# An expert kernel on one core: the first expert's start is put in another order

## The chip, the core and the metric

The kernel runs on one core of a Trainium2 chip. Its time is the device time of one execution in microseconds (us). TensorE (PE) multiplies, VectorE (DVE) and ScalarE (ACT) copy, convert and apply functions, GpSimd (POOL) computes too and issues the gathers, SyncE (SP) issues nearly all other DMAs. Each engine works through its own list of instructions in a fixed order and waits in it; so one instruction that waits holds up all that stand behind it in that list.

## The reference

Three stages on 2304 tokens of 512 numbers, in float32: an attention (two kinds, added), a dense product `((x @ w1) * (x @ w2)) @ w3 @ w_out`, and a mixture of eight experts in which each token goes to one of them. Cut to the part around the change:

```python
logits = x @ w_gate
e_idx = np.argmax(logits, axis=1)
probs = softmax(logits)
gate_w = probs[np.arange(N), e_idx]
eom = 1.0 / (1.0 + np.exp(-(x @ w_output_gate)))
for e in range(E):
    mask = e_idx == e
    h = np.maximum(x[mask] @ w1[e], 0.0)
    ye = h @ w2[e]
    out[mask] = gate_w[mask, None] * eom[mask, e, None] * ye
```

## The kernel before

Every float32 product is made of three matmuls (`mm3`, L418 to L420) of high and low parts: high by high, high by low, low by high. A weight piece of 128 x 1024 is loaded raw, ScalarE casts its high part (L737), and VectorE or GpSimd subtracts to give the low part (L739); `ew_load` and `ew_split` do this, four pieces for each of an expert's two matrices.

The dense stage works in groups of 384 tokens. `g2_step` makes its result y for 128 tokens and one half of the 512 columns: 24 matmuls into a PSUM bank, a copy into an SBUF buffer (L475 for the lower half, by ScalarE) and a store into the DRAM tensor `yd` (L476, by SyncE). Upper halves go to a second tensor, `yh`, too.

When all logits are known, tables of the tokens of each expert are made (`route_pos`, `route_tok`, `route_rank`, `route_idx`), and the experts follow in order of size, with `CAPS[0]` = 352 tokens in the first, that is three blocks of 128, 128 and 96. `x_gather` fetches the rows of an expert's tokens by an indirect DMA (L694, on GpSimd, one for each block), `x_prep` transposes them on PE (L712) and converts them to high and low (L716, ScalarE and VectorE). `ga_part` and `ga_step` multiply by the first matrix, in eight products f = 0 to 7 of 128 outputs each; `ga_out` applies ReLU (L765). `gb_step` multiplies by the second matrix. `o_step` scales a block by the gates and scatters it.

For the first expert the rows come in two parts, since the last lower halves of y are made last. The upper columns are gathered from `yh` (`x_gather(0, 1)`) while PE still makes lower halves. From them come the *upper halves* of six products of the first matrix (six matmuls each, without closing the sums). The lower columns are gathered from `yd` (`x_gather(0, 0)`) when the last store has landed, and then come the *lower halves* of those six products and the last two products whole. Between the upper halves and the lower rows stands `route_gtab` (L599): the matmul that puts the gates of the last group into the table; `route_gates` (L655, then L637 and L638) sums and picks the gates, which are first used when the first expert's output is scaled, in the second expert.

Order is written out by hand there: `ordered` chains PE's steps, `behind` makes a weight load wait for the first rows, `after` puts work behind a conversion, and a scheduler fills in the order on the other engines from its own estimate of times. PSUM: `at_psum` hands out two banks for transposes and small products, four banks hold f = 0 to 3, and two banks shared with `g2_step` hold f = 4 and 5.

Of the kernel before, what the change touches and what calls it, by code (L numbers as in the profile page):

```python
# [48 lines left out]
def attention_moe_kernel(ctx: ExitStack, tc: tile.TileContext, q, k, vw_in, v4_in, w1, w2, w3, w_out,  # L49
# [407 lines left out]

    def g2_step(g, t, hf):
        ps = ps2.tile([P, 512], F32, name="g2", tag="g2")
        n0, n1 = HALF[hf], HALF[hf + 1]  # L460
        for f in range(KF):
            c = slice(P * t, P * t + P)
            mm3(ps[:, 0:HN[hf]], hts[g, f][0][:, c], hts[g, f][1][:, c], wc[:, f, 0, n0:n1], wc[:, f, 1, n0:n1],
                f == 0, f == KF - 1)
        r0 = G * g + P * t
        n = DM // 2
        yn[0] += 1
        y = yb[:, yn[0] % 3, :]
        if hf == 1:
            if t == 0:  # L470
                lg[g] = mt([P, CPG, 2 * E], F32, "lg", bufs=2)
            nc.vector.tensor_copy(lg[g][:, t, :], ps[:, n:n + 2 * E])
            nc.vector.tensor_copy(y, ps[:, 0:n])
        else:
            nc.scalar.copy(out=y, in_=ps[:, 0:n])  # L475
        store = nc.sync.dma_start(out=yd[r0:r0 + P, n0:n0 + n], in_=y)  # L476
        if hf == 1:
            nc.sync.dma_start(out=yh[r0:r0 + P, :], in_=y)
        return store


    def at_psum():
        if psb is None:
            return psa.tile([P, 512], F32, name="at", tag="at")
        return psb.tile([P, 512], F32, name="tr", tag="tr", bufs=2)

    psb = None
    acc = mt([P, E], F32, "acc")
    tab = mt([P, 3, E, NC], F32, "tab")
# [257 lines left out]
    def ga_part(r, f, k0, k1, first, last):  # L747
        C = CAPS[r]
        hi, lo = ew[r, 0, f // 2]
        if first:  # L750
            if f < 4 or last:
                gp[f] = psb.tile([P, 512], F32, name="g1", tag="g1", bufs=4)
# [255 lines left out]
    for i in range(2):  # L1008
        ew_load(0, 0, i)
    ordered(g2_step, NG - 1, 0, 0)  # L1010
    rows = x_gather(0, 1)
    behind(rows, ew_load(0, 0, 2))
    behind(rows, ew_load(0, 1, 0, early[:, 0]))
    ew_split(0, 0, 0)
    ordered(g2_step, NG - 1, 1, 0)
    for b in range(NBLK[0] - 1):
        ordered(x_prep, 0, b, KD // 2, KD)
    ew_split(0, 0, 1)
    store = ordered(g2_step, NG - 1, 2, 0)
    with tc.issue_after(store.ins):  # L1020
        ew_load(0, 1, 1, early[:, 1])
    rows = x_gather(0, 0)
    behind(rows, ew_load(0, 0, 3))
    last = ordered(x_prep, 0, NBLK[0] - 1, KD // 2, KD)
    with after(last):
        ew_split(0, 0, 2)
        route_gate(NG - 1)
        rhs = mt([P, CPG, 2 * E * NC], F32R, "rhs", tag="W15")
        for c in range(CPG):
            gate_rhs(NG - 1, c, rhs[:, c])  # L1030
        ew_split(0, 1, 0)
    for f in range(6):
        ordered(ga_part, 0, f, KD // 2, KD, True, False)
    ordered(route_gtab, NG - 1, rhs)
    route_gates()
    with tc.issue_after(rows.ins):
        first = ew_split(0, 1, 1)
    for b in range(NBLK[0]):
        last = ordered(x_prep, 0, b, 0, KD // 2)
    with after(last):  # L1040
        ew_split(0, 0, 3)
    for i in range(2, 4):
        behind(rows, ew_load(0, 1, i, early[:, 2] if i == 2 else None))
    for r in range(E):
        for f in range(KF):
# [4 lines left out]
            if f % 2 == 0:  # L1050
                if r > 0:
                    ew_split(r, 1, f // 2)
                elif f < 4:
                    with after(last):
                        ew_split(r, 1, 2 + f // 2)
                if r + 1 < E:
                    ew_load(r + 1, 0, f // 2)
            if f % 2 == 1 and r > 0 and f // 2 < NBLK[r - 1]:
                ordered(o_step, r - 1, f // 2)
# [74 lines left out]
```

## Time and profile before

| what | us |
|---|---|
| median of three runs | 733.2 (728.99 to 734.5) |
| the profiled execution | 731.68 |
| its span, first to last instruction | 729.9 |
| PE busy | 695.8 (95%) |
| VectorE busy | 422.8 (58%) |
| GpSimd busy | 340.7 (47%) |
| ScalarE busy | 286.1 (39%) |

The span is what the profiler saw from the first to the last instruction; the execution's own time is 1.78 us longer. The mean granted clock of TensorE is 0.992 of its full 2.4 GHz; the lower level is 1.2 GHz, shown as 0.50. Matmuls overlap, so the length of one (0.32 us for 352 columns) is longer than the step from one to the next. A bracket behind an instruction tells how long its engine was idle before it and what ended that. DMA transfers themselves are not instructions: a row of SP or of an indirect DMA is the time of issuing it.

### The profile page before, as it was taken

To read this page: it belongs to the slowest core of one execution; us is meant where nothing else is said; L and a number is where in the kernel's file an instruction comes from. 1 tells how busy PE (TensorE), PEld (TensorE's weight loads), DVE (VectorE), ACT (ScalarE), POOL (GpSimd) and SP (SyncE) were. 2 spreads that over 40 slices of the span, in tenths; PEclk is the share of its full clock that TensorE was granted. 3 is DMA by queue.
4 is the path that set the end of the run, shared out by engine and by line. 5 is a ranking of instruction groups with operands and counts; after the bars stand their busy time and mean duration, and the time that the engine had idled before them with its cause. 6 is when DMAs were issued, how large, how long until landed. Compare 5 with 4: busy or idle time off the path is not lost.

```text
span 729.9 us, 14702 instructions
## 1 busy us (share of the span) xinstructions
PE 695.8 (95%) x5710; PEld 666.0 (91%) x5711; DVE 422.8 (58%) x884; ACT 286.1 (39%) x664; POOL 340.7 (47%) x339
## 2 busy tenths in 40 slices
PE   5887999999999999999999999989999999999995
PEld 3677989899999999999999999979999999999994
DVE  8997889854545446253242343575776656765830
ACT  3455435563444136135212121345353444544510
POOL 6975567873562157032011020166474655765511
PEclk9999999999999999999999999999999999999998
DMA  8978546363243043111100101665454744545301
GB/s 327 265 251 250 217 124 214 108 196 119 83 126 102 30 109 97 52 40 44 37 30 1 44 1 44 207 246 180 154 175 145 257 159 162 208 169 198 116 25 42
DMA packets 38266, 97.73 MB, mean 134 GB/s; under 512 B 6019, under 2 KB 12931, under 8 KB 38193
## 3 DMA queue, kind: packets, MB, share of 16 engines
q1 hardware_dynamic: 34768, 86.82, 36.5%
q0 software_dynamic: 3424, 9.93, 3.8%
q8 instruction: 46, 0.75, 0.5%
q14 instruction: 28, 0.22, 0.1%
HBM read 84.93 MB, written 12.29 MB: 133 GB/s over the span
## 4 chain that ended last, share of the span: by engine, by line
PE 77%; issue 7%; POOL 5%; DVE 5%; DMA 3%; ACT 1%; SPq 0%; POOLq 0%; DVEq 0%; ACTq 0%
PE g L418 23%; PE g L419 22%; PE g L420 22%; PE at L281 2%; DMA v<-in_v_dram 2%; PE tr L712 1%; PE at L221 1%; PE at L277 1%; DVE cv L139 1%; PE at L209 1%; PE tr L805 1%; DVE cv L138 1%; DVE wf L140 1%; PE at L265 1%; POOL out_dram L795 1%
## 5 line engine op out<-in xcount | busy, mean ns | idle before, releaser
L418 PE MATMUL g<-xh,W 128*128 128x384 f32 x384 | 131.9, 344 | 0.9 <-ACT a L446 0.9
L420 PE MATMUL g<-xh,W 128*128 128x384 f32 x384 | 129.2, 337 | 0.8 <-POOL W L397 0.7
L419 PE MATMUL g<-xl,W 128*128 128x384 f32 x384 | 129.2, 336 | 0.0
L739 DVE TENSOR_TENSOR W<-raw,W 128x1024 fp32r<-128x1024 f32 x32 | 87.7, 2771 | 32.8 <-ACT W L737 23.6
L739 POOL TENSOR_TENSOR W<-raw,W 128x1024 fp32r<-128x1024 f32 x29 | 82.9, 2879 | 36.0 <-ACT W L737 33.0
L418 PE MATMUL g<-xT,W 128*128 128x288 f32 (+6 forms) x256 | 81.5, 318 | 1.0 <-ACT xT L716 1.0
L419 PE MATMUL g<-xT,W 128*128 128x288 f32 (+6 forms) x256 | 79.8, 312 | 0.0
L420 PE MATMUL g<-xT,W 128*128 128x288 f32 (+6 forms) x256 | 79.6, 311 | 0.0
L451 POOL TENSOR_TENSOR h<-a,h 128x384 fp32r<-128x384 f32 x30 | 30.6, 1021 | 101.6 <-ACT h L449 101.6
L418 PEld LDWEIGHTS g<-xh,W 128*128 128x128 f32 x384 | 72.1, 188 | 2.6 <-ACT a L446 1.5
L420 PEld LDWEIGHTS g<-xh,W 128*128 128x128 f32 x384 | 72.1, 188 | 1.9 <-POOL W L397 1.8
L419 PEld LDWEIGHTS g<-xl,W 128*128 128x128 f32 x384 | 72.2, 188 | 0.1
L418 PE MATMUL g<-h,W 128*128 128x288 f32 (+5 forms) x224 | 69.9, 312 | 0.0
L418 PE MATMUL g<-wc,h 128*128 128x272 f32 (+1 forms) x240 | 68.7, 287 | 0.0
L419 PE MATMUL g<-wc,h 128*128 128x272 f32 (+1 forms) x240 | 68.3, 286 | 0.0
L419 PE MATMUL g<-h,W 128*128 128x288 f32 (+5 forms) x224 | 68.0, 304 | 0.0
L420 PE MATMUL g<-h,W 128*128 128x288 f32 (+5 forms) x224 | 68.0, 303 | 0.0
L420 PE MATMUL g<-wc,h 128*128 128x272 f32 (+1 forms) x240 | 67.9, 285 | 0.0
L737 ACT CAST W<-raw 128x1024 fp32r<-128x1024 f32 x61 | 59.8, 1046 | 9.0 <-DMA raw<-in_moe_w_dram 4.9
L447 DVE TENSOR_TENSOR a<-g,a 128x384 f32<-128x384 f32 x48 | 26.6, 554 | 55.6 <-PE g L420 50.3
L765 ACT ACTIVATE h<-g 128x288 fp32r<-128x288 f32 (+6 forms) x64 | 28.0, 437 | 77.1 <-PE g L420 71.5
L795 POOL DMA_INDIRECT out_dram<-orow,b_si x24 | 23.5, 978 | 62.9 <-DVE orow L794 59.3
(257 smaller groups left out, 1702.2 us busy)
## 6 DMA issues: line engine op xcount, KB each, us to landing
raw<-in_moe_w_dram SPq DMA_DIRECT2D x61, 512.0 KB
f64w<-in_moe_w_dram SPq DMA_DIRECT2D x16, 512.0 KB
f<-in_moe_w_dram SPq DMA_DIRECT2D x16, 512.0 KB
vw<-in_vw_dram SPq DMA_DIRECT2D x16, 384.0 KB
kc<-in_k_dram SPq DMA_DIRECT2D x16, 288.0 KB
qT<-in_q_dram SPq DMA_DIRECT2D x16, 288.0 KB
kz<-in_k_dram SPq DMA_DIRECT2D x32, 144.0 KB
v<-in_v_dram SPq DMA_DIRECT2D x16, 288.0 KB
```

The lines of the kernel that those rows point to most:

```text
L138: nc.vector.tensor_scalar(c, hi, 3, 0x3FFFFFF8, op0=ALU.logical_shift_left, op1=ALU.bitwise_and)
L139: nc.vector.scalar_tensor_tensor(c, hi, 0xC0000000, c, op0=ALU.bitwise_and, op1=ALU.bitwise_or)
L281: nc.tensor.matmul(xl[c // 3][64 * h:64 * h + 64, 96 * (c % 3):96 * (c % 3) + 96], vw[:, c, D * h:D * h + D], bd[:, 2 * c + h, :], start=T ...
L418: nc.tensor.matmul(ps, whi, xhi, start=first, stop=False)
L419: nc.tensor.matmul(ps, whi, xlo, start=False, stop=False)
L420: return nc.tensor.matmul(ps, wlo, xhi, start=False, stop=last)
L447: nc.vector.tensor_tensor(a, pp[1][:, 0:G], a, op=ALU.mult)
L451: eng.tensor_tensor(lo, a, hi.bitcast(F32), op=ALU.subtract)
L737: nc.scalar.copy(out=hi, in_=t)
L739: ins = eng.tensor_tensor(lo, t, hi.bitcast(F32), op=ALU.subtract)
L765: return nc.scalar.activation(out=t[:, 0, 0:C], in_=ps[:, 0:C], func=AF.Relu), nc.vector.scalar_tensor_tensor(t[:, 1, 0:C], ps[:, 0:C], 0. ...
L795: ins = nc.gpsimd.indirect_dma_start(out=out, out_offset=bass.IndirectOffsetOnAxis(ap=rt["si"][0:n, r, b:b + 1], axis=0), in_=t[0:n], in_o ...
```

## The change

Three things are put in another place; the arithmetic is the same.

- The last three stores of lower halves are issued by ScalarE in place of SyncE. The third block's upper rows are now converted in the middle of the last lower half (after five of its eight steps), not behind it.
- The fourth piece of the first matrix is loaded and split early, and a seventh upper half (f = 6) is computed before the lower rows; its sum is held in one of the two transpose banks (`tx`), so the transposes of the lower rows have one bank (`alone`). Of the second matrix only piece 0 is loaded early; pieces 1 to 3 are loaded behind the lower rows, and all four are split inside the product with the first matrix, after f = 0, 2, 4 and 6.
- `route_gtab` moves behind f = 1 of the first expert's product, `route_gates` behind f = 7.

```diff
-    def g2_step(g, t, hf):
+    def g2_step(g, t, hf, middle=None, queue=None):
...
+            if middle and f == KF // 2:
+                pe[0] = end.ins
+                middle()
...
-        store = nc.sync.dma_start(out=yd[r0:r0 + P, n0:n0 + n], in_=y)
+        store = (queue or nc.sync).dma_start(out=yd[r0:r0 + P, n0:n0 + n], in_=y)
...
-        return psb.tile([P, 512], F32, name="tr", tag="tr", bufs=2)
+        tr[0] += 1
+        tag = "tr" if alone[0] or tr[0] % 2 else "tx"
+        return psb.tile([P, 512], F32, name="tr", tag=tag, bufs=1)
...
-            if f < 4 or last:
+            if f == 6 and not last:
+                gp[f] = psb.tile([P, 512], F32, name="tr", tag="tx", bufs=1)
+            elif f < 4 or last:
...
-    ordered(g2_step, NG - 1, 0, 0)
+    ordered(g2_step, NG - 1, 0, 0, None, nc.scalar)
     rows = x_gather(0, 1)
-    behind(rows, ew_load(0, 0, 2))
+    for i in range(2, 4):
+        behind(rows, ew_load(0, 0, i))
     behind(rows, ew_load(0, 1, 0, early[:, 0]))
...
-    store = ordered(g2_step, NG - 1, 2, 0)
-    with tc.issue_after(store.ins):
-        ew_load(0, 1, 1, early[:, 1])
+    last = []
+    ordered(g2_step, NG - 1, 2, 0, lambda: last.extend(ordered(x_prep, 0, NBLK[0] - 1, KD // 2, KD)), nc.scalar)
     rows = x_gather(0, 0)
-    behind(rows, ew_load(0, 0, 3))
-    last = ordered(x_prep, 0, NBLK[0] - 1, KD // 2, KD)
     with after(last):
         ew_split(0, 0, 2)
+        ew_split(0, 0, 3)
...
-        ew_split(0, 1, 0)
-    for f in range(6):
+    alone[0] = True
+    for f in range(7):
         ordered(ga_part, 0, f, KD // 2, KD, True, False)
-    ordered(route_gtab, NG - 1, rhs)
-    route_gates()
-    with tc.issue_after(rows.ins):
-        first = ew_split(0, 1, 1)
...
+    for i in range(1, 4):
+        behind(rows, ew_load(0, 1, i, early[:, i] if i < 3 else None))
...
-                elif f < 4:
+                else:
                     with after(last):
-                        ew_split(r, 1, 2 + f // 2)
+                        split_ = ew_split(r, 1, f // 2)
+                        first = split_ if f == 2 else first
...
+            if r == 0 and f == 1:
+                ordered(route_gtab, NG - 1, rhs)
+            if r == 0 and f == KF - 1:
+                alone[0] = False
+                with after(last):
+                    route_gates()
```

The lists of the engines are what the scheduler makes of this. First ScalarE, from the first of the last three lower halves on. `COPY yb` is the copy of a lower half, `CAST xT` the conversion of a block of upper rows, `CAST W<-raw` the cast of a piece of the first matrix, `CAST W<-early` of the second, `r_pe` and `r_gs` are small exponentials of the gates. Before:

```order
L475 COPY yb<-g_5812 128x256
L475 COPY yb<-g_5852 128x256
L716 CAST xT<-tr 128x2x128 x2
L475 COPY yb<-g_5895 128x256
L716 CAST xT<-tr 128x2x96
L737 CAST W_5933<-raw 128x1024
L737 CAST W_5960<-early 128x1024
L568 ACTIVATE r_pe<-r_pe 128x24
L573 ACTIVATE r_gs<-r_gs 128x3
L737 CAST W_6017<-early 128x1024
```

and of the change:

```order
L480 DMA yd<-yb 128x256
L479 COPY yb<-g_5854 128x256
L723 CAST xT<-tr 128x2x128
L480 DMA yd<-yb 128x256
L723 CAST xT<-tr 128x2x128
L723 CAST xT<-tr 128x2x96
L744 CAST W_5932<-raw 128x1024
L744 CAST W_5936<-raw 128x1024
L575 ACTIVATE r_pe<-r_pe 128x24
L479 COPY yb<-g_5897 128x256
L580 ACTIVATE r_gs<-r_gs 128x3
L480 DMA yd<-yb 128x256
```

The copy of the last lower half (`g_5895` before, `g_5897` now) stood ahead of the third block's conversion and of both casts of weights; now it stands behind them.

Second ScalarE again, in the first expert's product behind the lower rows: `ACTIVATE h` is the ReLU of one product f. Of the change:

```order
L774 ACTIVATE h_6037<-g_5963 128x352
L744 CAST W_6040<-early 128x1024
L774 ACTIVATE h_6061<-g_5970 128x352
L774 ACTIVATE h_6075<-g_5977 128x352
L744 CAST W_6078<-early 128x1024
```

`W_6078` is piece 1 of the second matrix, now cast behind the third ReLU; before, it is `W_6017` of the first list, cast ahead of the lower rows.

Third GpSimd, from the last gather of lower rows (96 rows of 256) on. `TENSOR_TENSOR W` gives the low part of a piece, `xr<-yd,b_gi` with 512 columns are the gathers of the second expert's three blocks and of one of the third expert. Before:

```order
L694 DMA xr<-yd,b_g_5796 96x256
L739 TENSOR_TENSOR W_6018<-early,W_6017 128x1024
L694 DMA xr<-yd,b_gi 128x512 x2
L694 DMA xr<-yd,b_gi 80x512
L694 DMA xr<-yd,b_gi 128x512
L739 TENSOR_TENSOR W_6086<-raw,W_6085 128x1024
L739 TENSOR_TENSOR W_6188<-raw,W_6187 128x1024
```

and of the change:

```order
L701 DMA xr<-yd,b_g_5796 96x256
L746 TENSOR_TENSOR W_6079<-early,W_6078 128x1024
L701 DMA xr<-yd,b_gi 128x512 x2
L701 DMA xr<-yd,b_gi 80x512
L701 DMA xr<-yd,b_gi 128x512
L746 TENSOR_TENSOR W_6133<-raw,W_6132 128x1024
L746 TENSOR_TENSOR W_6188<-raw,W_6187 128x1024
```

The order is the same in both; what moved is what the first split (piece 1 of the second matrix) waits for, the cast by ScalarE, and with it all behind it, down to piece 3 (`W_6086`, now `W_6133`).

## Rows read from the trace of the kernel before

**Rows 1.** Stretches of 10 us (length; engines' busy us; clock; DMA share, GB/s).

```profile
70.00:80.00 10.00, 10.00 (x91) 9.56 (x89) 7.91 (x14) 6.37 (x17) 5.93 (x6) 0.83 0.87 324
...
470.00:480.00 10.00, 8.31 (x50) 7.23 (x48) 7.42 (x20) 4.58 (x9) 4.18 (x4) 1.00 0.58 194
480.00:490.00 10.00, 8.00 (x38) 7.58 (x39) 7.12 (x13) 5.40 (x10) 5.92 (x6) 0.83 0.84 308
```

**Rows 2.** PE by time (start, length; brackets: idle before), to the stall.

```profile
471.28 0.43 PE L418 MATMUL g<-xT,W 128*128 128x352 f32 x1 [0.56 <-ACT xT L716]
...
477.37 0.86 PE L599 MATMUL tr<-rhs,rb 128*128 128x288 f32 x3
...
479.32 0.41 PE L712 MATMUL tr<-ident,xr 128*128 128x128 f32 x2 [0.85 <-DMA xr<-yd,b_g]
481.57 0.38 PE L712 MATMUL tr<-ident,xr 96*128 96x96 f32 x2 [1.84 <-DVE xT L716]
```

**Rows 3.** PE in order of time, from the restart to the second matrix.

```profile
482.36 0.42 PE L418 MATMUL g<-xT,W 128*128 128x352 f32 x1 [0.41 <-ACT xT L716]
...
487.19 0.32 PE L418 MATMUL g<-xT,W 128*128 128x352 f32 x1
...
493.92 0.32 PE L418 MATMUL g<-h,W 128*128 128x352 f32 x1
```

**Rows 4.** ScalarE (ACT) in order of time.

```profile
470.63 0.37 ACT L475 COPY yb<-g 128x256 f32<-128x256 f32 x1 [2.35 <-issue]
...
472.74 1.05 ACT L737 CAST W<-early 128x1024 fp32r<-128x1024 f32 x1 [0.26 <-DMA early<-in_moe_w_dram]
...
487.39 0.47 ACT L765 ACTIVATE h<-g 128x352 fp32r<-128x352 f32 x1 [0.60 <-PE g L420]
```

**Rows 5.** VectorE (DVE) in order of time.

```profile
473.83 1.23 DVE L739 TENSOR_TENSOR W<-early,W 128x1024 fp32r<-128x1024 f32 x1
...
478.77 2.41 DVE L655 TENSOR_TENSOR b_gt<-tab 128x144 f32<-128x144 f32 x1
481.10 0.41 DVE L716 TENSOR_TENSOR xT<-tr,xT 128x256 fp32r<-128x256 f32 x1
```

**Rows 6.** The DMA queue of SyncE (SP) in order of time.

```profile
480.48 0.34 SPq L725 DMA_DIRECT2D raw<-in_moe_w_dram  x1
```

**Rows 7.** The last store of lower halves, by its tensor.

```profile
L476 SPq DMA_DIRECT2D yd<-yb x1: 331/331/331, 471.0 to 471.0; - x1
```

**Rows 8.** GpSimd (POOL) in order of time, to the last of the four gathers.

```profile
475.19 0.96 POOL L694 DMA_INDIRECT xr<-yd,b_g  x1 [10.21 <-DVE r_gs L574]
...
477.71 0.92 POOL L694 DMA_INDIRECT xr<-yd,b_g  x1 [0.30 <-issue]
478.65 2.35 POOL L739 TENSOR_TENSOR W<-early,W 128x1024 fp32r<-128x1024 f32 x1
481.16 0.98 POOL L694 DMA_INDIRECT xr<-yd,b_gi  x1 [0.16 <-issue]
...
484.90 0.96 POOL L694 DMA_INDIRECT xr<-yd,b_gi  x1 [0.30 <-issue]
```

**Rows 9.** POOL in order of time, its splits after the gathers.

```profile
488.87 2.42 POOL L739 TENSOR_TENSOR W<-raw,W 128x1024 fp32r<-128x1024 f32 x1 [3.01 <-DVE h L765]
495.59 5.74 POOL L739 TENSOR_TENSOR W<-raw,W 128x1024 fp32r<-128x1024 f32 x2 [4.30 <-ACT W L737]
```

**Rows 10.** SP and POOL in order of time: a lone store, the next gather.

```profile
458.80 0.32 SPq L476 DMA_DIRECT2D yd<-yb  x1
...
461.31 1.16 POOL L694 DMA_INDIRECT xr<-yh,b_gi  x1 [23.88 <-PE g L419]
```

**Rows 11.** Granted clock in stretches of half a microsecond.

```profile
483.50:484.00 0.50, 0.50 (x4) 0.50 (x3) 0.00 (x0) 0.00 (x0) 0.31 (x1) 0.50 1.09 442
...
486.50:487.00 0.50, 0.50 (x4) 0.50 (x3) 0.50 (x2) 0.29 (x1) 0.00 (x0) 0.72 1.10 434
```

**Rows 12.** PE's longest waits of the whole run (us in total, times, longest).

```profile
PE g L418 <- DVE wc L383: 6.5, 4, 3.9
```

More of the change, by code (lines that the diff above doesn't have):

```diff
@@ L1 @@
-from contextlib import ExitStack, contextmanager
+from contextlib import ExitStack, contextmanager, nullcontext
 import concourse.bass as bass
@@ L462, in g2_step @@
             c = slice(P * t, P * t + P)
-            mm3(ps[:, 0:HN[hf]], hts[g, f][0][:, c], hts[g, f][1][:, c], wc[:, f, 0, n0:n1], wc[:, f, 1, n0:n1],
-                f == 0, f == KF - 1)
+            with tc.issue_after(pe[0]) if middle and f > KF // 2 else nullcontext():
+                end = mm3(ps[:, 0:HN[hf]], hts[g, f][0][:, c], hts[g, f][1][:, c], wc[:, f, 0, n0:n1], wc[:, f, 1, n0:n1],
+                          f == 0, f == KF - 1)
+            if middle and f == KF // 2:
+                pe[0] = end.ins
+                middle()
         r0 = G * g + P * t
@@ L484, in at_psum @@
             return psa.tile([P, 512], F32, name="at", tag="at")
-        return psb.tile([P, 512], F32, name="tr", tag="tr", bufs=2)
+        tr[0] += 1
+        tag = "tr" if alone[0] or tr[0] % 2 else "tx"
+        return psb.tile([P, 512], F32, name="tr", tag=tag, bufs=1)
     psb = None
+    tr, alone = [0], [False]
     acc = mt([P, E], F32, "acc")
@@ L1009, in attention_moe_kernel @@
         ew_load(0, 0, i)
-    ordered(g2_step, NG - 1, 0, 0)
+    ordered(g2_step, NG - 1, 0, 0, None, nc.scalar)
     rows = x_gather(0, 1)
-    behind(rows, ew_load(0, 0, 2))
+    for i in range(2, 4):
+        behind(rows, ew_load(0, 0, i))
     behind(rows, ew_load(0, 1, 0, early[:, 0]))
     ew_split(0, 0, 0)
-    ordered(g2_step, NG - 1, 1, 0)
+    ordered(g2_step, NG - 1, 1, 0, None, nc.scalar)
     for b in range(NBLK[0] - 1):
@@ L1030, in attention_moe_kernel @@
             gate_rhs(NG - 1, c, rhs[:, c])
-        ew_split(0, 1, 0)
-    for f in range(6):
+    alone[0] = True
+    for f in range(7):
         ordered(ga_part, 0, f, KD // 2, KD, True, False)
-    ordered(route_gtab, NG - 1, rhs)
-    route_gates()
-    with tc.issue_after(rows.ins):
-        first = ew_split(0, 1, 1)
     for b in range(NBLK[0]):
         last = ordered(x_prep, 0, b, 0, KD // 2)
[L1040 to L1043, printed above, removed]
+    for i in range(1, 4):
+        behind(rows, ew_load(0, 1, i, early[:, i] if i < 3 else None))
+    first = None
     for r in range(E):
```

## The prediction

> **What bounds the kernel now.** I read the stretches of 10 us first: TensorE (PE) is busy all of its time in the second half of the run except where the first expert begins, 8.31 us of 10 and then 8.00, with the clock at 0.83 of full in the second [rows 1]. Everything the change touches lies there, so the most that it can win is what is lost there.
>
> Then PE in order of time. The upper halves of six products start at 471.28; the gate-table matmul (L599) follows at 477.37, and after it PE has only the transposes of the lower rows, which come one by one: the second block at 479.32 after an idle wait on its gather, the third at 481.57 after 1.84 us of waiting for VectorE [rows 2]. The lower halves start at 482.36 [rows 3]. From 478.2 to 482.36 PE does almost nothing. The half-microsecond stretches then show the granted clock at 0.50, the 1.2 GHz level, from 483.50, and 0.72 between 486.50 and 487.00 as it returns to 2.4 GHz [rows 11]: some 3.3 us at half speed, about 1.6 us lost.
>
> Third, what released the stall. The last copy of a lower half was made by ScalarE at 470.63 [rows 4], its store left SyncE's queue at 471.0 [rows 7], and GpSimd's first gather of lower rows started at 475.19, 4.2 us later; the third started at 477.71 [rows 8]. SyncE's next weight load, which waits for that third gather to land, left at 480.48 [rows 6], so landing is some 1.85 us after the gather's instruction ended at 478.63. VectorE was not free then: the sum of the gate tables (L655) ran from 478.77 to 481.18 and only then the second block's copy came, at 481.10 [rows 5]. So the stall has two limits, the store before the gathers and VectorE behind them.
>
> **The change, part by part.** The sum is made against the profiled execution, 731.68 us (span 729.9); the median of the runs is 733.2.
>
> *Stores from ScalarE.* In the order of ScalarE's instructions the third block's conversion and the casts of weight pieces 2 and 3 now stand ahead of the last copy of a lower half. A cast waits for its load. The second load behind the first gathers landed just before 472.74, when its cast (1.05) began after a wait on that DMA [rows 4]. Piece 3 is now that second load. Its cast ends at 473.79, so the copy (0.37) is made at about 473.9 rather than 470.63, and with one small exponential between (an estimate of 0.2, half of that copy) the store is issued at about 474.45 rather than 471.0. No DMA of the old kernel is issued by ScalarE; I bound the issue by SyncE's 0.32 to 0.34 [rows 6, 10], and nothing urgent is queued behind it there.
>
> What the store costs from there: with nothing ahead of it, a store issued at 458.80 was followed by a gather at 461.31, at most 2.51 [rows 10]; behind weight loads it was 4.2 [rows 7, 8]. Now the loads ahead of it have nearly all landed, so I take 2.5, and keep 4.2 as the upper end. The lower end is 1.85, what a gather takes to land: 0.65 less. First gather at 476.95, 1.76 later than before.
>
> *Gate tables out of the stall.* The third gather then starts 2.52 later as before [rows 8], at 479.47, and lands at about 482.24. VectorE now has only the three blocks' copies there. With one PSUM bank for the transposes instead of two, a block takes transposes (0.41) [rows 2], ScalarE's conversion (0.37, as the copies) and VectorE's (0.41) [rows 5], 1.2 to 1.3 us with the handing over, about the spacing of the gathers; I add 0.1. From the third block's transposes to the first lower half it was 481.57 to 482.36, 0.79. New restart: 483.1, **0.75 later**. VectorE's release gives back 1.1 of the 1.76.
>
> *The seventh upper half.* After the restart the old kernel ran 36 matmuls of lower halves and 24 of whole products in 11.56 us [rows 3]. At full clock the step between matmuls is 0.16: 42 of them from 487.19 to 493.92. Now six fewer follow the restart, **0.96 less**. The six run earlier under the wait for the rows, which is empty anyway. The gate-table matmul, three instructions formerly inside the stall (0.86 with overlap) [rows 2], now lies between lower halves: **0.5 more**, between 0.45 at full clock and 0.86. So the second matrix starts at about 494.2. The clock's loss of 1.6 after the stall stays, since the idle time is longer, not shorter.
>
> *What is late next.* The lower parts of pieces 1 and 3 of the second matrix are the price. Before, piece 1 was split at 478.65, during the stall, and the four gathers of the next rows followed from 481.16 to 485.86 [rows 8]; piece 3 was split at 488.87 [rows 9], five microseconds before it was due. Now ScalarE casts piece 1 only after the third ReLU, so GpSimd's queue, the gathers and piece 3 behind it all start later. The third ReLU was at 487.39 [rows 4], 5.03 after the restart; with the gate tables it is at restart + 5.5, 488.6. ReLU 0.4 and cast 1.05: 490.05. Split 2.35 to 492.4; from the old split's end at 481.00 to the last gather's end it took 4.86: 497.3; piece 3's split 2.42 [rows 9]: 499.7. PE needs it at the 21st matmul of the second matrix, 494.2 + 20 times 0.16 = 497.4. **PE waits 2.3 us.** Two splits beside a busy VectorE took 5.74, so 2.87 each [rows 9]; that is 0.5 more and the upper end by rows.
>
> The Trainium skill, SBUF — State Buffer, section Who interferes with whom, says that a VectorE instruction with two inputs in SBUF and a GpSimd one that reads SBUF exclude each other for the whole instruction. L655's 2.41 us, ending as GpSimd's split ends [rows 5, 8], agrees. By that rule VectorE's next split (1.23 alone [rows 5]) could hold piece 3 back by its whole length, and the sum would be 1.2 higher than below; by the 2.87 of the pair it would be 0.5 higher. I give that rule's full price one chance in ten within the forecast, since GpSimd's split was not held back by a whole instruction in the pair.
>
> *A second drop of the clock.* A wait of 3.9 us early in the run [rows 12] was followed by a mean clock of 0.83 in 70 to 80 [rows 1], and so was the stall here, of which the longest single idle piece is only 1.84 [rows 2]. The new wait of 2.3 is nearest to that piece. I take a drop, **1.6**; the lower end is none.
>
> The remaining edits cost nothing by themselves: the third block's transposes inside the last lower half take the 0.56 that PE waited at 471.28 away [rows 2], but only lengthen the stall; the gates are wanted by the first output block, in the second expert.
>
> Sum: 0.75 - 0.96 + 0.5 + 2.3 + 1.6 = +4.2, so 731.68 + 4.2 = **735.9 us**. Against the median of the runs that is 2.7 more, 0.4%. A measurement of this kernel tells about 1%, some 7 us, from no change.
>
> **Rivals.** *No new wait at the second matrix* (GpSimd's gathers go quicker, or PE itself is late enough): then only 0.75 - 0.96 + 0.5 = +0.3 is left, 732.0. For it: 2.3 us is the difference of two chains of some 14 us. Against it: every member of GpSimd's chain is a row.
>
> *It works as it reads*: the last store leaves as soon as PE has finished. Store at 471.4, gather at 473.9, restart at 480.0; idle for 2 us only, perhaps no drop of the clock (1.6). GpSimd's chain still ends some 2.3 too late. That is -2.4 - 0.46 - 1.6 + 2.3 = -2.2, 729.5; without the late chain 727.2. Against it stands the order on ScalarE. The Trainium skill, DMA: Bandwidth & Descriptors, section Issuing engines are not separate DMA queues, speaks against it too: another issuing engine saves the time of issuing and no more. No run here shows that yet.
>
> *Slower, the store stays behind the loads*: the first piece of the second matrix is now loaded third in a row, before the store. If the last gather but starts 4.2 us after the store instead of 2.5, all that follows the restart is 1.7 later: 737.6, or 738.1 with the longer split of 2.87. It decides from a store that takes over 3.5 us to the gather.
>
> **How the numbers follow.** Forecast with its wait at the second matrix: 0.55 (with the drop of the clock 0.33, at 735.9; without 0.22, at 734.3). No new wait 0.2; as it reads 0.1; store behind loads 0.15. The likeliest is 735.9. Runs of one kernel here lie between 728.99 and 734.5, so each case has some 2.5 us to either side: the range is 730.5 to 740. Faster by over 1% means under 725.9, which only the second rival with luck reaches: 0.03. Slower by over 1%, over 740.5: the third with all upper ends, 0.07. Within 1%: 0.90.
>
> **What would show it.** ScalarE's last copy of a lower half after two casts, near 474; the first gather of lower rows near 477; the restart near 483; VectorE's table sum out of the stall; GpSimd's split of piece 1 near 490 and of piece 3 ending near 500, with PE waiting for it in the second matrix; a second stretch of clock 0.50 after that. A gather of lower rows before 475.2, or no wait of PE on GpSimd near 497, makes the prediction wrong.

## The result and the profile after

The changed kernel takes 740.39 us (median of four runs, 737.6 to 743.01) against 733.52 for the kernel before. The ratio estimated from the runs, which isn't simply that of the medians, is 1.0107, with a 95% interval of 1.008 to 1.0133. A second measurement of the same kernel gave 738.42 us against 733.41 and 1.0078 (1.0049 to 1.0108). So by the medians it is slower by 5 to 7 us. The forecast was 735.9, in a range of 730.5 to 740.0: the sign and the places were right, the size was not.

The profiled execution took 743.01 us, 11.3 more than that of the kernel before (731.68). Not all of this is the change. VectorE's last addition to the token table is the same instruction in both kernels and precedes all that was moved. In these rows of VectorE (start, length, line, operation, tiles) it is found in the kernel before:

```profile
458.75 0.31 DVE L558 TENSOR_TENSOR tab<-tr,tab 128x144 f32<-128x144 f32 x1 [0.57 <-PE tr L556]
```

and after:

```profile
461.43 0.31 DVE L565 TENSOR_TENSOR tab<-tr,tab 128x144 f32<-128x144 f32 x1 [0.57 <-PE tr L563]
```

It is 2.68 us later, without the change's doing (in the profiles below it comes anywhere from 456.2 to 461.4). Times below are counted from this instruction, "the mark". PE after the change:

```profile
479.06 0.42 PE L418 MATMUL g<-xT,W 128*128 128x352 f32 x1 [0.83 <-ACT yb L479]
...
484.47 0.41 PE L719 MATMUL tr<-ident,xr 128*128 128x128 f32 x2 [3.22 <-DMA xr<-yd,b_g]
485.80 0.44 PE L719 MATMUL tr<-ident,xr 128*128 128x128 f32 x2 [0.92 <-DVE xT L723]
487.16 0.58 PE L719 MATMUL tr<-ident,xr 96*128 96x96 f32 x2 [0.92 <-DVE xT L723]
488.15 0.66 PE L418 MATMUL g<-xT,W 128*128 128x352 f32 x1 [0.41 <-ACT xT L723]
...
499.64 0.32 PE L418 MATMUL g<-h,W 128*128 128x352 f32 x1
...
506.71 0.55 PE L420 MATMUL g<-h,W 128*128 128x352 f32 x1 [3.72 <-POOL W L746]
...
521.71 0.31 PE L418 MATMUL g<-xT,W 128*128 128x336 f32 x1
```

The restart is at 488.15, the second matrix at 499.64 (against 482.36 and 493.92 [rows 3]), the second expert at 521.71; before, that was at 510.38:

```profile
510.38 0.31 PE L418 MATMUL g<-xT,W 128*128 128x336 f32 x1
```

| us | before | forecast | after |
|---|---|---|---|
| mark to restart | 23.61 | 24.36 | 26.72 |
| restart to second matrix | 11.56 | 11.1 | 11.49 |
| second matrix to second expert | 16.46 | 20.36 | 22.07 |
| second expert to the end | 219.56 | 219.56 | 219.56 |
| mark to the end | 271.2 | 275.4 | 279.8 |

Here "restart" is the first lower half, "second matrix" and "second expert" the first matmul of each. The last segment is alike to 0.01 us; the loss of 8.7 us is 3.1 up to the restart and 5.6 inside the second matrix. ScalarE:

```profile
474.40 1.05 ACT L744 CAST W<-raw 128x1024 fp32r<-128x1024 f32 x1 [1.70 <-DMA raw<-in_moe_w_dram]
477.58 1.05 ACT L744 CAST W<-raw 128x1024 fp32r<-128x1024 f32 x1 [2.14 <-DMA raw<-in_moe_w_dram]
478.66 0.35 ACT L479 COPY yb<-g 128x256 f32<-128x256 f32 x1
479.04 0.33 ACTq L480 DMA_DIRECT2D yd<-yb  x1
```

As foreseen, the last copy of a lower half comes behind the casts of pieces 2 and 3. But the second cast waited 2.14 us for its load, and the copy is made 17.2 us behind the mark, not 15.2 (before: 11.9 [rows 4]). PE waits for it too, 0.83 us: that copy frees the bank of the sixth upper half. GpSimd:

```profile
481.57 0.98 POOL L701 DMA_INDIRECT xr<-yd,b_g  x1 [13.93 <-DVE r_o L591]
...
495.57 2.40 POOL L746 TENSOR_TENSOR W<-early,W 128x1024 fp32r<-128x1024 f32 x1 [10.55 <-ACT W L744]
498.13 1.78 POOL L701 DMA_INDIRECT xr<-yd,b_gi  x1 [0.16 <-issue]
500.22 0.95 POOL L701 DMA_INDIRECT xr<-yd,b_gi  x1 [0.31 <-issue]
501.47 0.91 POOL L701 DMA_INDIRECT xr<-yd,b_gi  x1 [0.30 <-issue]
502.68 1.60 POOL L701 DMA_INDIRECT xr<-yd,b_gi  x1 [0.30 <-issue]
504.30 7.00 POOL L746 TENSOR_TENSOR W<-raw,W 128x1024 fp32r<-128x1024 f32 x3
```

From the store (479.04) to the gather (481.57) it is 2.53 us, as taken; the name in the bracket is that of an instruction that had ended 0.35 us earlier. Piece 1's split, four gathers and then piece 3's split stand as forecast, but the first and the fourth gather last 1.78 and 1.60 us, where they had taken 0.98 and 0.96 [rows 8]. Beside them, on VectorE:

```profile
497.44 1.62 DVE L746 TENSOR_TENSOR W<-early,W 128x1024 fp32r<-128x1024 f32 x1 [0.42 <-ACT W L744]
...
500.78 0.30 DVE L662 TENSOR_TENSOR b_gt<-tab 128x144 f32<-128x144 f32 x1
...
502.22 1.23 DVE L746 TENSOR_TENSOR W<-raw,W 128x1024 fp32r<-128x1024 f32 x1 [0.22 <-ACT W L744]
```

Both long gathers were issued while VectorE was in a split, and ended 0.85 and 0.83 us after it. The table sum, 2.41 us in the stall before [rows 5], takes 0.30. Last, the granted clock by half microseconds (length, busy time of PE, PEld, DVE, ACT and POOL with counts, clock, DMA share, GB/s):

```profile
486.50:487.00 0.50, 0.00 (x0) 0.00 (x0) 0.32 (x1) 0.15 (x1) 0.00 (x0) 0.50 0.00 0
...
492.50:493.00 0.50, 0.50 (x4) 0.50 (x4) 0.50 (x2) 0.14 (x1) 0.00 (x0) 0.50 1.07 442
493.00:493.50 0.50, 0.50 (x4) 0.50 (x3) 0.50 (x3) 0.00 (x0) 0.00 (x0) 0.79 1.02 418
...
507.00:507.50 0.50, 0.50 (x3) 0.50 (x3) 0.00 (x0) 0.00 (x0) 0.50 (x1) 0.50 0.27 107
```

The stretch at 1.2 GHz behind the stall lasts 6.8 us in place of 3.4 [rows 11], and one of 3.4 us follows the new wait.

### The profile page after: what moved, and what is told of

It reads as the page before. It is cut to its first block, busy times and chain, and to the rows that moved or that the text cites. A ratio compares the mean times of both kernels' runs of the same rounds, so it can differ in the third digit from the quotient of the medians.

```text
span 741.3 us, 14690 instructions
## 1 busy us (share of the span) xinstructions
PE 701.5 (95%) x5710; PEld 670.1 (90%) x5711; DVE 419.1 (57%) x884; ACT 286.2 (39%) x664; POOL 341.1 (46%) x339
## 4 chain that ended last, share of the span: by engine, by line
PE 71%; issue 6%; POOL 4%; DMA 4%; DVE 4%; ACT 0%; SPq 0%; POOLq 0%; DVEq 0%; ACTq 0%
PE g L418 21%; PE g L420 21%; PE g L419 20%; PE at L281 2%; PE tr L719 1%; PE at L221 1%; PE at L209 1%; PE tr L814 1%; POOL W L746 1%; PE at L277 1%; POOL xr L701 1%; DMA raw<-in_moe_w_dram 1%; POOL out_dram L804 1%; DVE cv L139 1%; PE at L265 1%
## 5 line engine op out<-in xcount | busy, mean ns | idle before, releaser
L746 DVE TENSOR_TENSOR W<-raw,W 128x1024 fp32r<-128x1024 f32 x32 | 84.9, 2685 | 33.3 <-ACT W L744 26.8
L418 PE MATMUL g<-xT,W 128*128 128x288 f32 (+6 forms) x252 | 80.5, 319 | 1.2 <-ACT yb L479 0.8
L419 PE MATMUL g<-xT,W 128*128 128x288 f32 (+6 forms) x252 | 78.5, 311 | 0.0
L420 PE MATMUL g<-xT,W 128*128 128x288 f32 (+6 forms) x252 | 78.3, 311 | 0.0
L744 ACT CAST W<-raw 128x1024 fp32r<-128x1024 f32 x61 | 59.9, 1047 | 10.9 <-DMA raw<-in_moe_w_dram 6.9
```

What stands on the lines that cost most here:

```text
L418: nc.tensor.matmul(ps, whi, xhi, start=first, stop=False)
L419: nc.tensor.matmul(ps, whi, xlo, start=False, stop=False)
L420: return nc.tensor.matmul(ps, wlo, xhi, start=False, stop=last)
L744: nc.scalar.copy(out=hi, in_=t)
L746: ins = eng.tensor_tensor(lo, t, hi.bitcast(F32), op=ALU.subtract)
```

## The experiments

One table for all of them. Times in us; copy (the last of a lower half) and restart are counted from the mark; "1.2 GHz" is the length of the stretches at that clock in this place, from rows of half a microsecond; the ratio is to the kernel before on the same chip (732.8 to 733.7 us in the later measurements), with its 95% interval. The edits follow below. What lies ahead of the mark differs between profiled runs by up to 5 us, so the segments tell more of this place than the times; but each row has its segments from one profile alone.

| kernel | copy | store to gather | gather to restart | restart | to 2nd matrix | to 2nd expert | 1.2 GHz | time | ratio |
|---|---|---|---|---|---|---|---|---|---|
| before | 11.9 | 4.15 | 7.2 | 23.6 | 11.6 | 16.5 | 3.4 | 733.5 | |
| after | 17.2 | 2.5 | 6.6 | 26.7 | 11.5 | 22.1 | 6.8 + 3.4 | 740.4 | 1.0107 (1.008, 1.0133) |
| again | 15.5 | 2.5 | 6.6 | 25.0 | 11.8 | 22.1 | 6.8 + 3.4 | 738.4 | 1.0078 (1.0049, 1.0108) |
| e2 | 15.4 | 2.5 | 6.8 | 25.1 | 11.0 | 16.5 | 6.8 | 732.9 | 1.0004 (0.9984, 1.0024) |
| s1 | 17.3 | 2.5 | 7.1 | 27.3 | 11.8 | 20.8 | 10.2 + 3.4 | 737.7 | 1.0064 (1.0039, 1.009) |
| s6 | 16.7 | 2.5 | 7.1 | 26.7 | 11.9 | 22.2 | 10.2 + 3.4 | 738.9 | 1.0069 (1.004, 1.0099) |
| s9 | 15.3 | 2.5 | 7.5 | 25.7 | 11.9 | 22.1 | 10.2 + 3.4 | 741.4 (one run) | |
| s8 | 15.4 | 2.5 | 6.9 | 25.2 | 10.9 | 20.9 | 6.8 + 3.4 | 739.4 | 1.0093 (1.0058, 1.0128) |
| e1 | 12.0 | 5.35 | 6.6 | 24.4 | 12.1 | 22.1 | 6.8 + 3.4 | 737.8 | 1.0071 (1.0047, 1.0095) |
| e4 | 16.5 | 2.5 | 7.1 | 26.5 | 12.0 | 22.1 | 10.2 + 3.4 | 738.8 | 1.008 (1.0059, 1.0102) |
| e3 | 12.0 | 5.1 | 6.8 | 24.4 | 11.1 | 16.5 | 6.8 | 732.5 | 1.0002 (0.9979, 1.0025) |
| s2 | 12.1 | 5.65 | 7.35 | 25.5 | 11.7 | 16.5 | 10.2 | 732.1 | 0.998 (0.9954, 1.0005) |
| s3 | 12.0 | 4.7 | 6.5 | 23.6 | 12.0 | 16.5 | 6.8 | 730.0 | 0.9966 (0.9943, 0.9989) |
| s4 | 12.0 | 5.4 | 6.55 | 24.4 | 11.2 | 16.6 | 6.8 | 732.4 | 0.9986 (0.9955, 1.0016) |
| s5 | 12.0 | 3.3 | 6.3 | 22.0 | 11.9 | 16.5 | 3.4 | 729.0 | 0.9962 (0.9939, 0.9984) |
| s7 | 12.0 | 3.1 | 6.0 | 21.5 | 10.3 | 16.5 | none | 729.2 | 0.996 (0.9934, 0.9987) |

### Once more

> The changed kernel once more, for its spread. If the late landing of piece 3 was particular to the first profile, its copy now comes 15.2 to 15.6 us behind the table addition and the restart at 25 us; if it is usual, 16.5 us or more and the restart at 26.5 or more. From the start of the second matrix to the second expert 22.1 us either way. Time 738 to 740 us.

This is the same kernel, without an edit. The copy came at 15.5 and the restart at 25.0. In eight of the profiles here the copy stands behind the casts: it comes at 15.3 to 15.5 in four of them (again, e2, s8, s9) and at 16.5 to 17.3 in the other four (after, s1, s6, e4). So the landing of piece 3, which decides it, varies by 2 us, and the first profile lies at the late end. The traces show what is late: a load has sixteen landing events, and in the four late profiles fifteen of piece 3's come by 14.0 to 14.5 us behind the mark and the last one alone 1.35 to 1.71 us after them; in the other four all sixteen lie within some half a microsecond. The stretch from the second matrix to the second expert takes the same 22.1.

### The wait in the second matrix

e2: VectorE takes piece 3's subtraction.

```diff
-eng = nc.vector if i % 2 != (r == 0 and m == 1) or (r == 0 and m == 0) else nc.gpsimd
+eng = nc.vector if i % 2 != (r == 0 and m == 1) or (r == 0 and m == 0) or (r, m, i) == (0, 1, 3) else nc.gpsimd
```

> The changed kernel, with the low part of the second matrix's piece 3 (first expert) made by VectorE instead of GpSimd. Theory A (that subtraction waits on GpSimd behind piece 1's and four gathers): the 3.7 us wait of PE in the second matrix goes, with the 3.4 us at half clock behind it (1.7 us): 735 us against 740.4. Theory B (something else would end the wait next: the cast, the rows of the second expert, VectorE's own queue): PE waits 1.5 us or more at the same place or within the next 10 us, and the time is 737.5 or more.

```profile
495.00 1.21 DVE L746 TENSOR_TENSOR W<-raw,W 128x1024 fp32r<-128x1024 f32 x1
```

This row of VectorE is the moved subtraction, done at 496.2. PE has no wait left there, nor the clock a second fall: 16.5 us as before, and the time is that of the kernel before, 732.9 (735 was expected). Theory A holds: the queue on GpSimd makes the wait.

s1: the subtraction stays on GpSimd, but ahead of the gathers.

```diff
-first = split_ if f == 2 else first
+first = split_ if f == 6 else first
...
-if f == 4 and r + 1 < E:
+if f == (6 if r == 0 else 4) and r + 1 < E:
```

> The changed kernel, with the four gathers of the second expert behind piece 3's subtraction on GpSimd, which stays there; copy and stores as in the change. Theory A (the wait in the second matrix is the queue on GpSimd, five instructions ahead of the subtraction): the subtraction follows piece 1's at once and ends about 5 us earlier, PE's wait falls from 3.7 us to under 0.5, the half clock behind it goes, and from the start of the second matrix to the second expert it takes 16.5 us instead of 22.1: some 734 us, as with the subtraction on VectorE. Theory B (GpSimd is too slow for this piece wherever it stands): a wait of 2 us or more is left. The gathers end some 2.5 us later than in the change; if the second expert then waits for its rows, a wait of 1 to 2 us appears at its first transposes.

PE's row with the wait that is left:

```profile
503.64 0.66 PE L719 MATMUL tr<-ident,xr 128*128 128x128 f32 x4 [2.42 <-DMA xr<-yd,b_gi]
```

The wait on the split is gone, and 2.42 us of waiting for the second expert's rows, with its fall of the clock, have taken its place. Theory A is right on the queue, but the conditional clause decides the time: in neither order is GpSimd done with both, the split and the gathers, before PE wants them.

s6: another instruction for VectorE's subtractions in that stretch.

```diff
-ins = eng.tensor_tensor(lo, t, hi.bitcast(F32), op=ALU.subtract)
+if eng is nc.vector and (r, m) in ((0, 1), (1, 0)):
+    ins = eng.scalar_tensor_tensor(lo, t, 0.0, hi.bitcast(F32), op0=ALU.add, op1=ALU.subtract)
+else:
+    ins = eng.tensor_tensor(lo, t, hi.bitcast(F32), op=ALU.subtract)
```

> The changed kernel, with VectorE's subtractions of the first expert's second matrix and the second expert's first made by another instruction (scalar_tensor_tensor, adding 0 first) with the same result; the order on all engines is as in the change. In the trace of the change the two of four gathers that were issued while VectorE was in such a subtraction took 1.78 and 1.60 us instead of 0.95 and ended 0.85 us after it. Theory A (the plain subtraction holds up the gather, and this made PE's wait 3.7 us rather than the 2.3 forecast): with the other instruction all four gathers take 0.9 to 1.0 us, GpSimd's subtraction starts 1.5 us earlier and PE waits 2.2 to 2.5 us; time 1.5 us less than the change's. Theory B (gathers are held up by any VectorE work, or by their own descriptors): two of them still take 1.6 us or more and the wait stays at 3.5 or more.

VectorE's instruction and the first gather beside it:

```profile
495.59 1.62 DVE L747 SCALAR_TENSOR_TENSOR W<-early,W 128x1024 fp32r<-128x1024 f32 x1 [0.42 <-ACT W L744]
```

```profile
496.28 1.79 POOL L701 DMA_INDIRECT xr<-yd,b_gi  x1
```

The gathers took 1.79, 0.95, 0.90 and 1.60 us and PE waited 3.72. Theory A as I put it, that the form of the instruction matters, fell (the other one, too, has two inputs in SBUF). Whether VectorE matters at all was open, hence the next two.

s9: three more subtractions beside gathers that had none.

```diff
+t3 = raws[0, 0, 3]
...
-for b in range(NBLK[0]):
-    last = ordered(x_prep, 0, b, 0, KD // 2)
+for _ in range(3):
+    more = nc.vector.tensor_tensor(ew[0, 0, 3][1], t3, ew[0, 0, 3][0].bitcast(F32), op=ALU.subtract)
+with tc.issue_after(more.ins):
+    for b in range(NBLK[0]):
+        last = ordered(x_prep, 0, b, 0, KD // 2)
```

> The changed kernel, with the low part of piece 3 of the first matrix made three times more on VectorE (the same values again), between the gate products and the conversions of the lower rows, where the gathers of the lower rows are issued and took 0.98, 0.95 and 0.91 us. Theory A (a gather issued while VectorE subtracts one piece in SBUF is held up until that ends): the second and third of them, or those that fall beside the three subtractions, take 1.5 to 2.2 us each. Theory B (VectorE has nothing to do with it): all three stay at 0.9 to 1.0 us. Either way the restart is later by what VectorE delays the conversions.

VectorE, then GpSimd:

```profile
479.40 3.74 DVE L1044 TENSOR_TENSOR W<-raw,W 128x1024 fp32r<-128x1024 f32 x3
```

```profile
478.60 0.98 POOL L701 DMA_INDIRECT xr<-yd,b_g  x1 [11.97 <-DVE r_o L591]
479.88 1.55 POOL L701 DMA_INDIRECT xr<-yd,b_g  x1 [0.30 <-issue]
481.74 0.92 POOL L701 DMA_INDIRECT xr<-yd,b_g  x1 [0.30 <-issue]
```

The three take 1.22 to 1.23 us each. The second gather was issued 0.48 us into the first of them and now took 1.55 us; the third, issued some 0.15 us before the end of the second, did not grow. One of two, then, where both were expected. Each ended 0.8 us after the subtraction in which it was issued, so one that is issued near its end loses nothing: what counts is the moment of issue.

s8: VectorE's subtractions in that stretch cut into eighths.

```diff
-ins = eng.tensor_tensor(lo, t, hi.bitcast(F32), op=ALU.subtract)
+n = 128 if (r, m, i) in ((0, 1, 2), (1, 0, 0), (1, 0, 1)) and eng is nc.vector else 1024
+for j in range(0, 1024, n):
+    ins = eng.tensor_tensor(lo[:, j:j + n], t[:, j:j + n], hi[:, j:j + n].bitcast(F32), op=ALU.subtract)
```

> The changed kernel, with VectorE's subtractions that fall beside the second expert's gathers (piece 2 of the second matrix, pieces 0 and 1 of the second expert's first) cut into eight of 128 columns each. If the hold is by instruction, the two long gathers take 1.0 to 1.2 us instead of 1.78 and 1.60, and PE's wait falls from 3.7 to 2.4 to 2.9 us. If it lasts as long as VectorE has such work, or isn't VectorE's, they stay at 1.6 us or more and the wait at 3.5 or more.

```profile
492.24 1.05 POOL L701 DMA_INDIRECT xr<-yd,b_gi  x1 [0.15 <-DVE W L748]
493.59 0.94 POOL L701 DMA_INDIRECT xr<-yd,b_gi  x1 [0.31 <-issue]
494.84 0.90 POOL L701 DMA_INDIRECT xr<-yd,b_gi  x1 [0.30 <-issue]
496.05 0.96 POOL L701 DMA_INDIRECT xr<-yd,b_gi  x1 [0.30 <-issue]
497.02 7.00 POOL L748 TENSOR_TENSOR W<-raw,W 128x1024 fp32r<-128x1024 f32 x3
```

```profile
499.44 0.43 PE L420 MATMUL g<-h,W 128*128 128x352 f32 x1 [2.33 <-POOL W L748]
```

The gathers are short again, and PE waits 2.33 us, the 2.3 of the forecast. The first gather is the test: it was issued in the second of eight small subtractions (492.16 to 492.44), ended 0.84 us after that one, and did not wait for the last, which ended at 493.65. The fourth no longer met a subtraction: VectorE's next began at 496.34, 0.29 us after it. Together with s9: a gather that is issued during a VectorE subtraction is held until that instruction ends. The time does not show the gain: the clock falls behind a wait of 2.33 us as behind 3.72, and the 1.4 us that are left are less than the interval.

### The restart

e1: the copy and store of the last lower half ahead of the casts.

```diff
-ordered(g2_step, NG - 1, 2, 0, lambda: last.extend(...), nc.scalar)
+store = ordered(g2_step, NG - 1, 2, 0, lambda: last.extend(...), nc.scalar)
...
-with after(last):
+with after(last), tc.issue_after(store.ins):
     ew_split(0, 0, 2)
     ew_split(0, 0, 3)
```

> The changed kernel, with the copy and store of the last lower half put ahead of the casts of pieces 2 and 3 on ScalarE; nothing else moves. Theory A (the restart is late because that copy stands behind two casts that wait for loads): the copy runs at once when PE ends the half, some 5 us earlier against the table addition ahead of it (L565); the 0.83 us wait of the sixth upper half goes; the lower rows are there when PE ends the seventh upper half, so that only the transposes and conversions of three blocks (3.7 us) stay in the gap, and the restart comes 4 us earlier against L565 (22.7 instead of 26.7 us behind it). The stretch at half clock behind the restart shrinks from 6.8 to 3.4 us, another 1.7 us. Sum: about 735 us against 740.4. Theory B (the loads of this stretch delay store, gather and rows whatever ScalarE's order is): the restart gains 1 us or less, 739 to 740 us.

ScalarE's store and GpSimd's first gather of lower rows:

```profile
469.98 0.33 ACTq L480 DMA_DIRECT2D yd<-yb  x1
```

```profile
475.32 1.22 POOL L701 DMA_INDIRECT xr<-yd,b_g  x1 [11.57 <-DVE r_o L591]
```

The store left 12.4 us behind the mark, 5.2 and 3.5 us earlier than in the two profiles of the change, but its gather followed after 5.35 us instead of 2.5. The restart gained 2.3 against the first and 0.6 against the second. Theory A holds on the order and fails on the size: an earlier store is a longer one. Of its sixteen landing events fourteen came by 15.5 us behind the mark, the last at 16.9, and the gather 0.9 after that; so 1.4 us of the 5.35 hang on the last two alone. What delays them stays open.

e4: the stores on SyncE, the copy where the change has it.

```diff
-ordered(g2_step, NG - 1, 0, 0, None, nc.scalar)
+ordered(g2_step, NG - 1, 0, 0)
```

(and so for the other two)

> The changed kernel with the three stores issued by SyncE again; ScalarE's copies stay where they are. Theory A (it is the place of the copy, not the queue of the store, that made the restart late): cast of piece 3, copy and restart stay within 0.7 us of the changed kernel's (26.7 us from L565 to the restart) or later, if a store stands behind loads on SyncE; 740 to 741 us. Theory B (a store from ScalarE beside the weight loads slowed the load of piece 3, of which one DMA engine was 1.7 us late): the cast of piece 3 comes 1.7 us earlier, with the restart; 738.7 us or less.

The cast of piece 3 waited 1.57 us for its load, the copy came at 16.5 and the restart at 26.5: no gain of 1.7. Piece 3 is late with the stores on SyncE too, so ScalarE's queue isn't needed for it. With a copy that varies by 2 us without any edit, one profile can't tell whether the queue adds something.

e3: the diffs of e1 and e2 together.

> The changed kernel with both edits: the last copy and store ahead of the casts, and piece 3's low part by VectorE. If both causes are independent, the gains add: 740.4 - 5.5 - 5.4 = 729.5 us, 4 us under the kernel before (733.5). If the clock loss is shared or a new wait comes, 732 to 735.

732.5 us, where 729.5 was to come if the gains added: the first does not add to the second. Behind the restart it is e2's; up to it, 0.7 us less than e2.

s2: e3, with the stores on SyncE (e4's diff).

> The kernel with both edits (copy ahead of the casts, piece 3 by VectorE; store to gather 5.1 us, restart 24.4 us behind the table addition), with the three stores on SyncE again. Theory A (a store issued early waits for the weight loads that move at that time, whichever engine issues it): store to gather 4.5 to 5.5 us, restart within 0.5 us, the time within 1 us of it. Theory B (the store takes 5 us because ScalarE issues it; SyncE's took 4.15 us in the kernel before): store to gather 4.2 us or less, restart about 1 us earlier.

```profile
470.27 0.33 SPq L480 DMA_DIRECT2D yd<-yb  x1
```

```profile
475.92 1.23 POOL L701 DMA_INDIRECT xr<-yd,b_g  x1 [11.91 <-DVE r_o L591]
```

5.65 us from SyncE: theory A, a little over its 5.5. The restart is 1.1 us later than e3's rather than within 0.5. In s2 (5.65 us, for 5.1 to 5.4 from ScalarE) and e4 (2.5 us, as from ScalarE) another issuing engine makes no store faster. The Trainium skill, DMA: Bandwidth & Descriptors, section Issuing engines are not separate DMA queues, says that DMAs run on the same 16 DMA engines whichever engine started them, which agrees.

s3: e3, with one load less in that stretch.

```diff
-behind(rows, ew_load(0, 1, 0, early[:, 0]))
...
-for i in range(1, 4):
+for i in range(4):
     behind(rows, ew_load(0, 1, i, ...))
```

> The kernel with both edits, with the early load of the second matrix's piece 0 put behind the lower rows; the stretch of the last store then has two weight loads instead of three. Theory A (the store shares the DMA engines with three loads of 512 KB): store to gather falls from 5.1 us to 3 or 4, and the restart comes 1 to 2 us earlier (22.5 to 23.4 us behind the table addition). Theory B (the loads don't hold the store): store to gather stays above 4.8 us. Against it: piece 0 lands later; if its split is late, the second matrix waits.

Store to gather fell to 4.7 us, between the two theories, and the restart came at 23.6; the second matrix does not wait for piece 0 (16.5 us).

s5: s3, with six upper halves, two transpose banks and one load less again.

```diff
-for i in range(2, 4):
-    behind(rows, ew_load(0, 0, i))
+behind(rows, ew_load(0, 0, 2))
...
+behind(rows, ew_load(0, 0, 3))
...
-ew_split(0, 0, 3)
...
-alone[0] = True
-for f in range(7):
+for f in range(6):
...
+with after(last):
+    ew_split(0, 0, 3)
```

> The kernel with both edits and piece 0 of the second matrix loaded late (last store to gather 4.7 us, restart 23.6 us behind the table addition, 730.0 us), with six upper halves again: piece 3 of the first matrix is loaded behind the lower rows too, and the lower rows have two transpose banks. Theory A (every load taken from this stretch brings the store forward, and one bank costs the transposes 0.9 us of waiting for conversions): store to gather 3 to 4 us, gather to restart 6.0 instead of 6.5, restart 21.5 to 22.5; the six matmuls come back, 1 us, and the piece must be there 8 us behind the restart: 729 to 730 us. Theory B (the seventh half pays for itself): restart 23.0 or later and 731 or more.

The store and the gather in s5:

```profile
469.66 0.33 ACTq L480 DMA_DIRECT2D yd<-yb  x1
```

```profile
472.92 0.96 POOL L701 DMA_INDIRECT xr<-yd,b_g  x1 [9.49 <-DVE r_gs L584]
```

With three loads ahead of the store it takes 5.1 to 5.65 us to the gather (e1, e3, s2, s4), with two 4.7, with one 3.3. The step from three to two was smaller than s3 expected, but every step goes one way, and the kernel before (two loads ahead of its last store, 4.15) fits: a store shares the transfers with the loads of its stretch. s5 restarts at 22.0, earlier than all but s7, and its ratio to the kernel before is 0.9962, some 2.8 us. Only 1.3 us of that lie behind the mark in the profiles (269.9 us to the end, for 271.2); and s3, at 0.9966, is 0.5 us longer there than the kernel before. So what these edits gain in time isn't shown. Of the change s5 keeps the ScalarE stores and the late gate tables, with the edits of e1 and e2; what it drops is the seventh half and the early loads.

### The gate tables and the clock

s4: e3, with the gate-table matmuls back in the stall.

```diff
+ordered(route_gtab, NG - 1, rhs)
 for b in range(NBLK[0]):
     last = ordered(x_prep, 0, b, 0, KD // 2)
...
-if r == 0 and f == 1:
-    ordered(route_gtab, NG - 1, rhs)
```

> The kernel with both edits, with the gate-table matmuls back ahead of the lower rows, in the gap; the sums of the gates stay late. Theory A (behind the restart the matmuls cost what they last, 0.46 us, or 0.92 at half clock; in the gap they are free): from the restart to the second matrix 10.2 to 10.6 us instead of 11.1. Theory B (in the gap they hold the one transpose bank that is left): the restart comes 0.5 us or more later and the gain is gone.

Neither theory: the restart is the same, and so is the way to the second matrix, 11.15 for 11.11. The stretch at 1.2 GHz began 0.9 us later and so lay 0.9 us longer over the matmuls behind the restart, half of which is lost: it ate the 0.46.

s7: s5, with ten matmuls of no use in the gap.

```diff
+ordered(fill, 10)
 for b in range(NBLK[0]):
     last = ordered(x_prep, 0, b, 0, KD // 2)
```

> The kernel with six upper halves, with ten more matmuls of 352 columns (1.6 us, their result is not used) between the last upper half and the first transposes of the lower rows. Theory A (the granted clock falls because PE idles there): the stretch at half clock behind the gap gets shorter by 3.4 us or goes, 1 to 1.7 us less than without them. Theory B (the transposes and their waits are enough for the clock to fall): the stretch stays, and the time is the same or up to 1 us longer.

Stretches of PE in s5 and in s7:

```profile
480.00:490.00 10.00, 10.00 (x56) 10.00 (x55) 6.93 (x9) 7.01 (x12) 3.83 (x2) 0.84 1.00 404
```

```profile
480.00:490.00 10.00, 9.59 (x60) 9.26 (x59) 5.94 (x10) 6.98 (x13) 2.41 (x2) 1.00 0.91 354
```

The clock stays at 2.4 GHz, and from restart to second matrix it takes 10.3 us instead of 11.9. Theory A: with the gap filled the clock does not fall. The times, 729.2 and 729.0, do not show these 1.6 us; their intervals overlap.

## Why the prediction was wrong

**Right.** The order on ScalarE, copy behind two casts; store to gather 2.5, with some luck, since it was taken from a gather of another tensor, `yh` [rows 10]; the table sum out of the stall; PE's wait on piece 3's split at the 21st matmul; a second fall of the clock. The rivals "no new wait" and "as it reads" both fell, the second even where its order is made (e1: restart 24.4 us behind the mark, where 480.0 would be 21.2).

**Wrong: the wait of 2.3 us.** The step that failed is "from the old split's end at 481.00 to the last gather's end it took 4.86". It took 6.3 (497.97 to 504.28), since two gathers were issued inside VectorE's splits: 1.45 us more, and PE's wait grew by 1.42, from 2.3 to 3.72. With short gathers it is 2.33 (s8). With the fall of the clock the segment was forecast at 20.4 and took 22.1: 1.7 of the error. The trace of the kernel before had such a gather already, a little later, 0.82 us past the end of VectorE's two splits:

```profile
496.50 5.93 DVE L739 TENSOR_TENSOR W<-raw,W 128x1024 fp32r<-128x1024 f32 x2 [1.36 <-ACT W L737]
```

```profile
501.49 1.76 POOL L694 DMA_INDIRECT xr<-yd,b_gi  x1 [0.16 <-issue]
```

The forecast had weighed the rule of the Trainium skill, SBUF — State Buffer, section Who interferes with whom, for GpSimd's split alone, at one chance in ten. That rule is on a VectorE instruction with two inputs in SBUF beside a GpSimd one that reads SBUF. It would hold up a gather too, if issuing one reads its indices there; no run here shows by what the gather is held. The same section says that `tensor_tensor` did not stall DMA in a probe, and infers that it leaves free what issuing needs. Here a gather that was issued inside a `tensor_tensor` took 1.55 to 1.80 us for 0.95; the measurement decides.

**Wrong: piece 3 as "that second load".** Its cast was taken to end 15.0 us behind the mark, as that of the second load of before did, and the copy to follow at 15.15. In eight profiles the copy came at 15.3 to 17.3: four of them bear the term out within 0.4 us, the first profile of the change is among the others, 2.1 us late. What was late is one landing event of sixteen, by 1.7 us in the first profile; what held that one up stays open, and e4 shows that it happens without stores from ScalarE. Gather to restart took 0.4 more than the forecast. Together the restart was forecast 0.75 later and came 3.1 later; in the second profile 1.35 later.

**Wrong: the clock's loss "stays".** Its stretch doubled behind the longer stall, 6.8 for 3.4 us: part of it lay over the transposes, some 5.1 us behind the restart, where it had been all of 3.4. The way to the second matrix took 0.4 longer than forecast.

Sum of the errors: 2.4 + 0.4 + 1.7 = 4.5, and 4.2 forecast make 8.7, the difference of the two profiles behind the mark. By medians the change cost 6.9 us and then 5.0, against 2.7 forecast from the median. In the second profile the restart and the way to the second matrix are 0.6 and 0.7 us over the forecast, the segment behind them again 1.7, so the held gathers are the largest part there. What the seventh half, the single transpose bank and the late table sum are worth by themselves was not tested.

**The rival "store stays behind the loads"** was not what happened, 2.53 us, but its mechanism is real: it holds for every early store (5.1 to 5.65), and is why putting the copy right brings so little.

## What to carry to other kernels

When an instruction is moved on GpSimd, look at what VectorE does at the new time: price gathers by their neighbours, not only by their own rows. A store on the critical path gained little from an earlier issue while big loads were in flight (e1); with fewer loads it gained more (s3, s5). And a copy that feeds such a store and frees a bank should not stand behind casts that wait for loads: here its time varied by 2 us with one load's landing.

## What had not been expected of the hardware

A gather's issue of 0.95 us took 1.55 to 1.8 when it began well within a VectorE subtraction of 1.2 to 1.6 us, and 1.05 when that was cut into eighths. The other way round the hold was longer still. In s8, VectorE's row

```profile
496.34 7.83 DVE L748 TENSOR_TENSOR W<-raw,W 128x128 fp32r<-128x128 f32 x2 [0.22 <-ACT W L744]
```

shows two subtractions of 128 columns, 0.28 each elsewhere, taking 7.83 us: the second began while GpSimd issued a gather, 0.47 us before its three subtractions of 7.00 us, and ended only behind them. And of the sixteen landing events of a 512 KB load the last came up to 1.7 us behind the other fifteen, and the cast that waited for the load began only then. Last, ten useless matmuls in a gap kept TensorE at 2.4 GHz, where the same gap without them was followed by 3.4 us at 1.2.
